# Bias of the mixing stage added by VectorE with the third product, in the first eight of twelve groups

## The chip, the cores and the metric

One core of a Trainium2 chip runs the whole kernel. Its engines work side by side, each through its own queue in a fixed order: TensorE (PE in the rows, its weight loads PEld), VectorE (DVE), ScalarE (ACT), GpSimd (POOL), and SyncE (SP), which issues most transfers. The metric is the device time of one execution in microseconds; of three runs of the kernel before, the median is 1185.93 us (1185.71 to 1186.15).

## The reference, cut to what matters

The input is `x`, two sequences of 3008 rows by 256. The first layer mixes in the frequency domain; two gated layers follow, each on all 6016 rows.

```python
X = np.fft.rfft(x, axis=1)
Xr, Xi = X.real, X.imag
Yr = Xr @ w_r - Xi @ w_i + b_r
Yi = Xr @ w_i + Xi @ w_r + b_i
Yr = np.sign(Yr) * np.maximum(np.abs(Yr) - lam, 0.0)     # lam = 0.01
Yi = np.sign(Yi) * np.maximum(np.abs(Yi) - lam, 0.0)
y = np.fft.irfft(Yr + 1j * Yi, n=3008, axis=1)
...
h = x @ w_in;   x = (h * np.clip(h + 3, 0, 6) / 6) @ w_out       # 256 -> 2048 -> 256
g = x @ w_gate; x = (g * sigmoid(g) * (x @ w_val)) @ w_out2      # 256 -> 1536 -> 256
```

The change lies in the two `+ b` terms.

## The kernel before, in words

**The stages.** From 0 to about 190 us the kernel does the first layer, and from group 8 on the first blocks of the second layer between its pieces. The rest, to 1185 us, is the two gated layers. The transform is split: `pre` makes a first transform of the rows (line 328 or 330), its results go to memory (`Bd`) and come back as tiles `z`; then twelve groups `(b, Q)`, six to a sequence, pass through three steps; the inverse of the first transform (`post`, line 573) reads what they wrote to memory (`Cd`).

**A group's three steps.** All matrices are kept as a high and a low part, so that a product is three matmuls (`xh·wl`, `xh·wh`, `xl·wh`).

- `s2` (two halves): line 397 makes the group's frequencies in PSUM. ScalarE copies one part out (`sum`, L403) and casts the high part (`X`, L404), VectorE forms the difference (L405) and the low part (L132). In the following step, `then` makes the high and low part of the difference (ScalarE L410, VectorE L132).
- `ln` (two halves, `h` = 0 and 1): the complex product with the weights in three real products of 2 x 3 matmuls each (L441 to L443). Two go to the two halves of the PSUM tile `p3`, the third to `p4`. Ahead of them line 446 fills `p3` with the bias (plus lam) by a product of `ones` with `shift`. ScalarE copies `p4` to `k1` (L452), VectorE adds it to both halves (`yb`, L454). In the following step, `then` does the threshold: ScalarE L459 makes `yc` from `yb`, VectorE L460 makes `yp` from both.
- `ia` (line 471): multiplies `yp` of both halves back; ScalarE copies the result to `cs` (L474), POOL sends it to `Cd`.

**What sets the order.** Nothing is scheduled by the machine: each engine's queue holds what the code issues, in that order. For groups 2 to 7 the order on TensorE is `ln(p,0)`, `s2(p+1)`, `ia(p-1)`, `ln(p,1)`, then the next group; `run` puts the deferred halves (`then`) of one step behind the matmuls of the next. `ln` also makes a step of `conv1.step()` in groups 1 to 7: it converts the second layer's weights from 64-bit words, with one or two ScalarE casts (L170, L191) and up to four short VectorE operations (L175, L188, L179, L195). `flush` then issues the deferred halves. So VectorE's queue holds, over and over: four conversions, `yb(p,0)`, the first half of `s2`, `yp(p,0)`, the second half, the low parts, four conversions, `yb(p,1)`, `yp(p,1)`.

**PSUM.** Eight banks are used in turn. From group 8 (`FROM`) on, five are left, since three hold sums of the second layer.

**SBUF.** `b_st`, which holds the bias as it comes from memory, is one of three buffers of the ring `r`, which also holds `yb` and `yc`. It is needed only until `shift` is made of it (L297, L298, L300).

Of the kernel before, what the change touches and what calls it, by code (L numbers as in the profile page):

```python
# [9 lines left out]
F32 = mybir.dt.float32  # L10
# [4 lines left out]
ALU = mybir.AluOpType  # L15
# [5 lines left out]
SEQ, DIM, NB = 3008, 256, 2  # L21
# [5 lines left out]
LAM = 0.01  # L27
# [58 lines left out]
def fourier_moe_kernel(ctx: ExitStack, tc: tile.TileContext, x, lin, bias, w1, w2, fwd1, inv2, fwd2,  # L86
                       inv1, out):
    nc = tc.nc

    def pool(stack, name, side):  # L90
        return stack.enter_context(tc.tile_pool(name=name, bufs=1, side=side))
# [39 lines left out]
    def low(o, full, hi):  # L131
        nc.vector.tensor_tensor(out=o, in0=full, in1=hi.bitcast(F32), op=ALU.subtract)  # L132
# [89 lines left out]
    ap_ = pool(attn_stack, "attn", "right")  # L222
    linh = ap_.tile([128, 3, 2, DIM], F32R, name="linh")
    linl = ap_.tile([128, 3, 2, DIM], F32R, name="linl")
    shift = ap_.tile([128, 2 * DIM], F32R, name="shift")
    ones = ap_.tile([128, 128], F32R, name="ones")
# [8 lines left out]
    def load_x(k):  # L235
        t, src = room[k], x[k * 2 // NT, k % (NT // 2)]
        if k == 0:
            for n in range(4):
                c = slice(n * TC // 2, (n + 1) * TC // 2)
                nc.sync.dma_start(t[:QP, c], src[:, c])  # L240
        else:
            nc.sync.dma_start(t[::2], src[:64])
            nc.sync.dma_start(t[1::4], src[64:])
# [17 lines left out]
    p = [psf[0]([128, 512], f"p0_{n}") for n in range(2)]  # L261
# [4 lines left out]

    def prepare():
        lin_st = ap_.tile([128, 2, 2, DIM], F32, tag="z", name="lin_st", bufs=3)
        b_st = spread("b_st")
        nc.gpsimd.dma_start(lin_st, lin)  # L270
        nc.gpsimd.dma_start(b_st[:64], bias)
        for h in range(2):
            nc.gpsimd.memset(room[5][:, h * TC : (h + 1) * TC], 0.0)
        load_x(5)
        load_m(0, 0)
        o = spread("o_st")[:, :128]
        nc.gpsimd.memset(o, 0.0)
        for r in (0, 32):
            nc.gpsimd.memset(o[r : r + 1], 1.0)
        nc.gpsimd.tensor_copy(ones, o)  # L280
        nc.gpsimd.tensor_copy(shift[64:], zeros[64:])
        w = [lin_st[:, k] for k in range(2)]

        def mixed(op):
            w.append(spread("mixed").rearrange("p (a b) -> p a b", b=DIM))
            nc.vector.tensor_tensor(out=w[-1], in0=w[1], in1=w[0], op=op)

        def hi(i, k):
            nc.scalar.copy(linh[:, i], w[k])

        def lo(i, k):
            low(linl[:, i], w[k], linh[:, i])

        def shifts(i):
            b = b_st[:64]
            if i == 0:
                nc.vector.tensor_scalar(b, b, LAM, None, op0=ALU.add)  # L297
                nc.scalar.copy(shift[:64], b)  # L298
            else:
                low(shift[32:64], b[32:], shift[32:64])  # L300

        amid.update({
            6: [lambda: mixed(ALU.subtract), lambda: hi(2, 0)], 7: [lambda: mixed(ALU.add), lambda: hi(0, 2)],
            8: [lambda: lo(2, 0), lambda: shifts(0)], 9: [lambda: lo(0, 2), lambda: hi(1, 3)],
            10: [lambda: lo(1, 3), lambda: shifts(1)]})

    amid = {}

    def spread(name):
        return xs_p.tile([128, 2 * DIM], F32, tag="r", name=name, bufs=3)  # L310
# [60 lines left out]
    def table(tag, src, Q, name, bufs):  # L371
        t = ap_.tile([128, 4, 128], F32, tag=tag, name=name, bufs=bufs)
        nc.sync.dma_start(t, src[:, Q * 512 : (Q + 1) * 512].rearrange("r (g c) -> r g c", g=4))
        return t

    def load_m(b, Q):
        if (b, Q) not in m_t:
            m_t[b, Q] = table("m", fwd2, Q, f"m{b}_{Q}", 3)
# [38 lines left out]
    def flush():  # L417
        while due:
            due.pop(0)()
# [8 lines left out]
    def ln(b, Q, h):  # L428

        if (b, Q) not in n_t:  # L430
            n_t[b, Q] = table("n", inv1, Q, f"n{b}_{Q}", 3)
        if 0 < ORDER.index((b, Q)) < FROM:
            conv1.step()
        flush()
        xs = [t[:, :, :, h * 128 : (h + 1) * 128] for t in X[b, Q]]

        def product(o, form, k, start):
            for dh in range(2):
                xh, xl = (t[:, dh, form] for t in xs)
                wh, wl = linh[:, k, dh], linl[:, k, dh]  # L440
                nc.tensor.matmul(o, xh, wl, start=start and dh == 0, stop=False, skip_group_check=not start)  # L441
                nc.tensor.matmul(o, xh, wh, start=False, stop=False, skip_group_check=not start)  # L442
                nc.tensor.matmul(o, xl, wh, start=False, stop=dh == 1, skip_group_check=not start)  # L443

        p = psf[0]([128, 2, DIM], f"p3_{b}_{Q}_{h}")
        nc.tensor.matmul(p.rearrange("r c d -> r (c d)"), ones, shift, start=True, stop=True)
        product(p[:, 1], 0, 0, False)
        product(p[:, 0], 1, 1, False)
        p1 = psf[0]([128, DIM], f"p4_{b}_{Q}_{h}")
        product(p1, 2, 2, True)  # L450
        k1 = ap_.tile([128, DIM], F32, tag="k1", name=f"k1{b}_{Q}_{h}", bufs=2)
        nc.scalar.copy(k1, p1)  # L452
        yb = xs_p.tile([128, 2, DIM], F32, tag="r", name=f"yb{b}_{Q}_{h}", bufs=3)
        nc.vector.tensor_tensor(out=yb, in0=p, in1=k1.unsqueeze(1).to_broadcast([128, 2, DIM]), op=ALU.add)  # L454
        yc = xs_p.tile([128, 2, DIM], F32, tag="r", name=f"yc{b}_{Q}_{h}", bufs=3)
        y = yp[b, Q, h] = ap_.tile([128, 2, DIM], F32, tag="yp", name=f"yp{b}_{Q}_{h}", bufs=3)

        def then():
            nc.scalar.activation(yc, yb, AF.Relu, bias=edges)  # L459
            nc.vector.scalar_tensor_tensor(out=y, in0=yb, scalar=0.0, in1=yc, op0=ALU.min, op1=ALU.add)  # L460

        later.append(then)
# [19 lines left out]
    ORDER = [(b, Q) for b in range(NB) for Q in range(NQ)]  # L482
    FROM = 8
# [11 lines left out]
    def L(p):  # L495
        return [lambda h=h: ln(*ORDER[p], h) for h in range(2)]
# [682 lines left out]
    for q in range(len(quads2) + 1):  # L1179
        if q < len(quads2) and quads2[q][1] == 0 and quads2[q][0] + 1 < len(pairs):  # L1180
            p = quads2[q][0] + 1
# [50 lines left out]
```

## Time and profile before

| | us |
|---|---|
| median of three runs | 1185.93 |
| the profiled execution's own time | 1187.32 |
| its span, first to last instruction | 1185.5 |
| TensorE busy in the span | 1176.2 (99%) |
| VectorE busy | 915.3 (77%) |
| ScalarE busy | 780.9 (66%) |

The page names TensorE as busy nearly all the time and puts 94% of the chain that ended last on it, under a granted clock of 1.00. Matmuls overlap in the profile: one has a duration of 280 or 400 ns, but the next starts after some 120 or 230 ns. What one matmul is worth is therefore read from the distance of starts or from the chain, not from its duration. The average also hides the stages: what holds TensorE up between 30 and 115 us is read from that stretch alone.

### The profile page before, as it was taken

To read this page: it belongs to the slowest core of one execution; us is meant where nothing else is said; L and a number is where in the kernel's file an instruction comes from. 1 tells how busy PE (TensorE), PEld (TensorE's weight loads), DVE (VectorE), ACT (ScalarE), POOL (GpSimd) and SP (SyncE) were. 2 spreads that over 40 slices of the span, in tenths; PEclk is the share of its full clock that TensorE was granted. 3 is DMA by queue.
4 is the path that set the end of the run, shared out by engine and by line. 5 is a ranking of instruction groups with operands and counts; after the bars stand their busy time and mean duration, and the time that the engine had idled before them with its cause. 6 is when DMAs were issued, how large, how long until landed. Compare 5 with 4: busy or idle time off the path is not lost.

```text
span 1185.5 us, 17927 instructions
## 1 busy us (share of the span) xinstructions
PE 1176.2 (99%) x6576; PEld 979.5 (83%) x6576; DVE 915.3 (77%) x1629; ACT 780.9 (66%) x1432; POOL 58.0 (5%) x91
## 2 busy tenths in 40 slices
PE   9999999999999999999999999999999999999998
PEld 3898887888888888888899888888888888888997
DVE  5688985898989989989987666766766766766665
ACT  3577775688777777777777555655655655655554
POOL 4010004500000000000000000000000000000000
PEclk9999999999999999999999999999999999999999
DMA  8898534964472673643553544644644644644551
GB/s 300 299 323 224 169 84 133 311 231 151 131 259 93 189 247 106 201 158 142 204 185 133 178 155 155 228 155 158 231 156 160 229 160 160 226 160 160 200 195 71
DMA packets 69208, 219.63 MB, mean 185 GB/s; under 512 B 6672, under 2 KB 29200, under 8 KB 57296
## 3 DMA queue, kind: packets, MB, share of 16 engines
q1 hardware_dynamic: 66144, 209.28, 51.4%
q0 software_dynamic: 2688, 9.05, 2.6%
q8 instruction: 51, 0.84, 0.3%
q14 instruction: 37, 0.30, 0.1%
q10 hardware_dynamic: 288, 0.16, 0.0%
HBM read 172.07 MB, written 46.40 MB: 184 GB/s over the span
## 4 chain that ended last, share of the span: by engine, by line
PE 94%; DVE 3%; DMA 2%; ACT 1%; issue 1%; POOL 0%; SPq 0%; ACTq 0%; POOLq 0%; DVEq 0%
PE acc L127 12%; PE acc L129 12%; PE acc L128 12%; PE P L933 8%; PE P L935 8%; PE P L934 8%; PE Tb L935 4%; PE Tb L933 4%; PE Tb L934 4%; PE Q L933 2%; PE Q L935 2%; PE Q L934 2%; PE p L471 2%; PE p L397 2%; PE p L442 1%; PE p L443 1%
## 5 line engine op out<-in xcount | busy, mean ns | idle before, releaser
L990 ACT COPY hold<-P 128x512 f32<-128x512 f32 (+1 forms) x224 | 128.7, 575 | 78.5 <-PE P L935 77.4
L613 ACT CAST gated<-r 128x512 fp32r<-128x512 f32 (+1 forms) x160 | 98.1, 613 | 64.9 <-DVE r L981 53.7
L132 DVE TENSOR_TENSOR gated<-s,gated 128x512 fp32r<-128x512 f32 (+1 forms) x144 | 97.4, 676 | 49.7 <-ACT gated L1117 49.7
L985 DVE TENSOR_TENSOR hold<-Q,hold 128x512 f32<-128x512 f32 (+1 forms) x112 | 76.1, 679 | 67.6 <-PE Q L935 55.3
L132 DVE TENSOR_TENSOR gated<-r,gated 128x512 fp32r<-128x512 f32 (+1 forms) x160 | 107.9, 674 | 21.6 <-ACT gated L613 18.3
L127 PE MATMUL acc<-gated,w_o 128*128 128x512 f32 (+1 forms) x320 | 123.9, 387 | 0.0
L128 PE MATMUL acc<-gated,w_o 128*128 128x512 f32 (+1 forms) x320 | 123.1, 385 | 0.0
L129 PE MATMUL acc<-gated,w_o 128*128 128x512 f32 (+1 forms) x320 | 123.0, 384 | 0.0
L129 PE MATMUL acc<-gated,slot 128*128 128x512 f32 (+1 forms) x288 | 111.1, 386 | 0.0
L127 PE MATMUL acc<-gated,slot 128*128 128x512 f32 (+1 forms) x288 | 111.0, 385 | 0.1
L128 PE MATMUL acc<-gated,slot 128*128 128x512 f32 (+1 forms) x288 | 110.9, 385 | 0.0
L985 DVE TENSOR_TENSOR hold<-P,hold 128x512 f32<-128x512 f32 (+1 forms) x112 | 75.8, 677 | 39.3 <-PE P L935 39.3
L1157 ACT ACTIVATE s<-hold 128x512 f32<-128x512 f32 (+1 forms) x72 | 44.9, 623 | 85.6 <-DVE hold L985 85.6
L977 ACT ACTIVATE r<-hold,consts 128x512 f32<-128x512 f32 (+1 forms) x120 | 85.7, 715 | 17.3 <-DVE hold L985 15.1
L985 DVE TENSOR_TENSOR hold<-Tb,hold 128x512 f32<-128x512 f32 (+1 forms) x112 | 76.0, 678 | 26.5 <-PE Tb L935 19.4
L933 PE MATMUL P<-xo,slot 128*128 128x512 f32 (+1 forms) x240 | 91.7, 382 | 0.2
L934 PE MATMUL P<-xo,slot 128*128 128x512 f32 (+1 forms) x240 | 91.5, 381 | 0.0
L935 PE MATMUL P<-xo,slot 128*128 128x512 f32 (+1 forms) x240 | 91.4, 381 | 0.0
L1117 ACT CAST gated<-s 128x512 fp32r<-128x512 f32 (+1 forms) x144 | 88.1, 612 | 1.5 <-DVE s L1172 1.2
L981 DVE SCALAR_TENSOR_TENSOR r<-r,hold 128x512 f32<-128x512 f32 (+1 forms) x120 | 80.9, 674 | 4.5 <-ACT r L977 3.4
L1162 ACT ACTIVATE s<-hold 128x512 f32<-128x512 f32 (+1 forms) x72 | 45.0, 625 | 51.5 <-DVE hold L985 51.5
L990 ACT COPY hold<-Tb 128x512 f32<-128x512 f32 (+1 forms) x112 | 64.8, 578 | 7.8 <-PE Tb L935 0.4
(190 smaller groups left out, 2865.8 us busy)
## 6 DMA issues: line engine op xcount, KB each, us to landing
slot<-Wd SPq DMA_DIRECT2D x72, 1152.0 KB, 5.1
slot<-Sd SPq DMA_DIRECT2D x40, 896.0 KB, 4.7
st<-in_w SPq DMA_DIRECT2D x68, 256.0 KB, 5.0
Wd<-slot SPq DMA_DIRECT2D x12, 1152.0 KB, 5.1
z<-Bd SPq DMA_DIRECT2D x12, 512.0 KB, 5.6
Cd<-cs POOLq DMA_DIRECT2D x24, 256.0 KB, 4.1
Xd<-x SPq DMA_DIRECT2D x20, 256.0 KB, 3.0
raw<-Xd SPq DMA_DIRECT2D x5, 1024.0 KB, 7.5
```

Of the source, the lines that this page charges most:

```text
L127: nc.tensor.matmul(o, wl, xh, start=start, stop=False)
L128: nc.tensor.matmul(o, wh, xh, start=False, stop=False)
L129: nc.tensor.matmul(o, wh, xl, start=False, stop=stop)
L132: nc.vector.tensor_tensor(out=o, in0=full, in1=hi.bitcast(F32), op=ALU.subtract)
L613: nc.scalar.copy(hi[:, :n], g[:, :n])
L933: nc.tensor.matmul(o, wl, x[m][:, 0, :n], start=start, stop=False, skip_group_check=not start)
L934: nc.tensor.matmul(o, wh, x[m][:, 1, :n], start=False, stop=False, skip_group_check=not start)
L935: nc.tensor.matmul(o, wh, x[m][:, 0, :n], start=False, stop=True, skip_group_check=not start)
L977: nc.scalar.activation(r[:, :n], x[:, :n], AF.Relu, bias=three)
L985: nc.vector.tensor_tensor(out=h, in0=x[:, :n], in1=c, op=ALU.add)
L990: nc.scalar.copy(c, x[:, :n])
L1117: nc.scalar.copy(hi[:, :nb], t[:, :nb])
```

## The change

In groups 0 to 7 (`early`) the product with `ones` is left out, and the first product into each half of `p3` starts its sum anew. ScalarE's copy of `p4` to `k1` is left out as well. Instead VectorE makes two additions where it made one: first `p4` (read twice, by broadcast) plus the bias plus lam, from SBUF, into `yb`; then `p3` plus `yb` into `yb`. For this the bias stays in SBUF on all 128 partitions, in a buffer of its own (`b_st` leaves the ring `r`), and the array on the host has 128 equal rows instead of 64. Groups 8 to 11 are as before, so `ones` and `shift` are still made.

```diff
     def prepare():
-        b_st = spread("b_st")
+        b_st = ap_.tile([128, 2 * DIM], F32, name="b_st")
+        edge_b.append(b_st.rearrange("p (c d) -> p c d", d=DIM))
         nc.gpsimd.dma_start(lin_st, lin)
-        nc.gpsimd.dma_start(b_st[:64], bias)
+        nc.gpsimd.dma_start(b_st, bias)
...
-                nc.vector.tensor_scalar(b, b, LAM, None, op0=ALU.add)
+                nc.vector.tensor_scalar(b_st, b_st, LAM, None, op0=ALU.add)
                 nc.scalar.copy(shift[:64], b)
...
         p = psf[0]([128, 2, DIM], f"p3_{b}_{Q}_{h}")
-        nc.tensor.matmul(p.rearrange("r c d -> r (c d)"), ones, shift, start=True, stop=True)
-        product(p[:, 1], 0, 0, False)
-        product(p[:, 0], 1, 1, False)
+        early = ORDER.index((b, Q)) < FROM
+        if not early:
+            nc.tensor.matmul(p.rearrange("r c d -> r (c d)"), ones, shift, start=True, stop=True)
+        product(p[:, 1], 0, 0, early)
+        product(p[:, 0], 1, 1, early)
         p1 = psf[0]([128, DIM], f"p4_{b}_{Q}_{h}")
         product(p1, 2, 2, True)
-        k1 = ap_.tile([128, DIM], F32, tag="k1", name=f"k1{b}_{Q}_{h}", bufs=2)
-        nc.scalar.copy(k1, p1)
         yb = xs_p.tile([128, 2, DIM], F32, tag="r", name=f"yb{b}_{Q}_{h}", bufs=3)
-        nc.vector.tensor_tensor(out=yb, in0=p, in1=k1.unsqueeze(1).to_broadcast([128, 2, DIM]), op=ALU.add)
+        if early:
+            nc.vector.tensor_tensor(out=yb, in0=p1.unsqueeze(1).to_broadcast([128, 2, DIM]), in1=edge_b[0], op=ALU.add)
+            nc.vector.tensor_tensor(out=yb, in0=p, in1=yb, op=ALU.add)
+        else:
+            k1 = ap_.tile([128, DIM], F32, tag="k1", name=f"k1{b}_{Q}_{h}", bufs=2)
+            nc.scalar.copy(k1, p1)
+            nc.vector.tensor_tensor(out=yb, in0=p, in1=k1.unsqueeze(1).to_broadcast([128, 2, DIM]), op=ALU.add)
```

VectorE's queue in the kernel before, from the second half of group 4 to the first half of group 5 (names end in sequence, group and half; `wt`, `head`, `st` and `w1` belong to the conversion of weights):

```order
L454 TENSOR_TENSOR yb0_4_1_891<-p3_0_4_1_868,k10_4_1_889 128x512
L460 SCALAR_TENSOR_TENSOR yp0_4_1_894<-yb0_4_1_891,yc0_4_1_893 128x512
L195 TENSOR_TENSOR w1_c_733<-wt_735,w1_c_733 128x256
L175 TENSOR_SCALAR wt_902<-head_864 128x256
L188 SCALAR_TENSOR_TENSOR wt_860<-head_781,wt_860 128x256
L179 SCALAR_TENSOR_TENSOR wt_902<-st_741,wt_902 128x256
L454 TENSOR_TENSOR yb0_5_0_933<-p3_0_5_0_910,k10_5_0_931 128x512
```

The same place in the changed kernel:

```order
L456 TENSOR_TENSOR yb0_4_1_870<-p4_0_4_1_863,b_st_161 128x512
L457 TENSOR_TENSOR yb0_4_1_870<-p3_0_4_1_850,yb0_4_1_870 128x512
L467 SCALAR_TENSOR_TENSOR yp0_4_1_874<-yb0_4_1_870,yc0_4_1_873 128x512
L195 TENSOR_TENSOR w1_c_719<-wt_721,w1_c_719 128x256
L175 TENSOR_SCALAR wt_882<-head_846 128x256
L188 SCALAR_TENSOR_TENSOR wt_842<-head_765,wt_842 128x256
L179 SCALAR_TENSOR_TENSOR wt_882<-st_727,wt_882 128x256
L456 TENSOR_TENSOR yb0_5_0_910<-p4_0_5_0_903,b_st_161 128x512
L457 TENSOR_TENSOR yb0_5_0_910<-p3_0_5_0_890,yb0_5_0_910 128x512
```

Nothing changes its place on VectorE; each `yb` has become two rows, the second of which reads what the first wrote.

TensorE's queue in the kernel before, where `ia` of group 3 ends and `ln` of group 4 begins its second half:

```order
L471 MATMUL p5_0_3_0_842<-yp0_3_1_769,n0_3_650 128x256
L471 MATMUL p5_0_3_1_843<-yp0_3_1_769,n0_3_650 128x256
L446 MATMUL p3_0_4_1_868<-shift_121,ones_122 128x512
L441 MATMUL p3_0_4_1_868<-linl_120,X0_4_691 128x256
L442 MATMUL p3_0_4_1_868<-linh_119,X0_4_691 128x256
```

In the changed kernel:

```order
L478 MATMUL p5_0_3_0_824<-yp0_3_1_753,n0_3_638 128x256
L478 MATMUL p5_0_3_1_825<-yp0_3_1_753,n0_3_638 128x256
L442 MATMUL p3_0_4_1_850<-linl_120,X0_4_677 128x256
L443 MATMUL p3_0_4_1_850<-linh_119,X0_4_677 128x256
L444 MATMUL p3_0_4_1_850<-linh_119,X0_4_677 128x256
```

The row of 512 columns is gone, and the group's first product of 256 columns follows `ia` directly.

## Rows read from the trace of the kernel before

**Rows 1.** The page, busy us of each engine, share of the span, instructions.
```profile
PE 1176.2 (99%) x6576; PEld 979.5 (83%) x6576; DVE 915.3 (77%) x1629; ACT 780.9 (66%) x1432; POOL 58.0 (5%) x91
```

**Rows 2.** Busy time by stretch of one group (us, instructions), granted clock, DMA share, GB/s.
```profile
54.30:64.80 10.50, 10.50 (x78) 8.79 (x77) 6.86 (x14) 6.78 (x16) 1.80 (x3) 1.00 0.99 327
82.20:90.90 8.70, 8.70 (x73) 8.02 (x72) 7.67 (x19) 6.57 (x18) 1.26 (x2) 1.00 1.00 336
99.60:108.30 8.70, 8.70 (x72) 7.89 (x70) 7.62 (x18) 6.40 (x17) 1.26 (x2) 1.00 0.95 185
```

**Rows 3.** One line's instructions: count, ns min/median/max, first and last start, form.
```profile
L446 PE MATMUL p<-shift,ones x24: 389/400/793, 32.8 to 178.6; 128*128 128x512 f32 x24
...
L452 ACT COPY k<-p x24: 351/373/394, 35.8 to 181.2; 128x256 f32<-128x256 f32 x24
...
L454 DVE TENSOR_TENSOR yb<-p,k x24: 681/691/693, 36.2 to 181.6; 128x512 f32<-128x512 f32 x24
...
L297 DVE TENSOR_SCALAR b_st<-b_st x1: 411/411/411, 24.2 to 24.2; 64x512 f32<-64x512 f32 x1
```

**Rows 4.** The chain that ended last, by time: start us, us on the chain, what.
```profile
31.10 5.96 DMA z<-Bd
...
79.73 0.23 PE p L446
79.96 0.12 PE p L441
...
85.83 0.43 PE p L446
```

**Rows 5.** VectorE's timeline: start us, us, line, operation, [idle before <- releaser].
```profile
61.54 0.36 DVE L175 TENSOR_SCALAR wt<-head 128x256 uint32<-128x256 uint32 x1
61.94 0.42 DVE L179 SCALAR_TENSOR_TENSOR wt<-st,wt 128x256 uint32<-128x256 uint32 x1
...
80.17 0.69 DVE L454 TENSOR_TENSOR yb<-p,k 128x512 f32<-128x512 f32 x1
81.66 0.69 DVE L460 SCALAR_TENSOR_TENSOR yp<-yb,yc 128x512 f32<-128x512 f32 x1 [0.79 <-ACT yc L459]
...
83.47 0.68 DVE L454 TENSOR_TENSOR yb<-p,k 128x512 f32<-128x512 f32 x1
84.07 0.41 DVE L405 TENSOR_TENSOR sum<-p,sum 128x256 f32<-128x256 f32 x1
...
88.86 0.69 DVE L454 TENSOR_TENSOR yb<-p,k 128x512 f32<-128x512 f32 x1
```

**Rows 6.** Who VectorE waited for, 60 to 115 us: total us, times, longest.
```profile
DVE yp L460 <- ACT yc L459: 4.7, 6, 0.8
DVE X L132 <- ACT X L410: 2.8, 6, 1.1
DVE xa L132 <- ACT xa L586: 0.8, 1, 0.8
DVE yb L454 <- ACT k L452: 0.6, 2, 0.4
DVE sum L405 <- ACT X L404: 0.5, 2, 0.3
```

**Rows 7.** TensorE's timeline where the transform of `post` ends; columns as in rows 5.
```profile
113.05 0.50 PE L129 MATMUL ph<-xa,w_c 128*128 128x512 f32 x1 [0.20 <-DVE xa L132]
```

**Rows 8.** ScalarE's timeline in group 4; columns as in rows 5.
```profile
80.90 0.73 ACT L459 ACTIVATE yc<-yb,consts 128x512 f32<-128x512 f32 x1 [0.76 <-DVE yb L454]
86.82 0.43 ACT L410 CAST X<-sum 128x256 fp32r<-128x256 f32 x1
```

**Rows 9.** The chain at the end of the first layer; columns as in rows 4.
```profile
186.63 1.98 PE p L471 x16
188.60 1.07 ACT cs L474 x2
...
190.58 3.71 DMA Cd<-cs
...
195.46 0.50 PE acc L127
```

**Rows 10.** VectorE's timeline, a slower operation of the same size later; columns as in rows 5.
```profile
215.03 0.96 DVE L132 TENSOR_TENSOR gs<-r,gs 128x512 fp32r<-128x512 f32 x1 [1.69 <-ACT gs L613]
```

More of the change, by code (lines that the diff above doesn't have):

```diff
@@ L305, in prepare @@
             10: [lambda: lo(1, 3), lambda: shifts(1)]})
-    amid = {}
+    amid, edge_b = {}, []
     def spread(name):
@@ L1193 @@
     xp = np.pad(xp, ((0, 0), (0, QP - QN), (0, 0))).reshape(NB, QP, NJ // 8, 8 * DIM).transpose(0, 2, 1, 3)
-    bias = np.tile(np.concatenate([b_r, b_i]), (64, 1))
+    bias = np.tile(np.concatenate([b_r, b_i]), (128, 1))
     def rows(w):
```

## The prediction

> **What bounds the kernel now.** I read the page's busy times first: TensorE 99%, its weight loads 83%, VectorE 77% [rows 1]. That is an average over stages, and the changed instructions all lie between 32 and 108 us, so the next view is the busy time by stretches of one group, to see who has room there. In every stretch TensorE is busy throughout and the granted clock is 1.00. VectorE goes from 6.86 of 10.50 us in an early stretch to 7.67 of 8.70 in a later one [rows 2]. The chain by time shows how TensorE's work lines up: up to 37.1 us it waits for a transfer, from then on one matmul follows the other, 0.12 us for one of 256 columns and 0.23 us for the product with ones [rows 4]. VectorE's timeline and the list of its waits then show what its apparent room consists of [rows 5, 6], and TensorE's timeline after the last changed group shows the place that decides: at 113.05 us TensorE itself waits for VectorE's `xa` [rows 7]. So at that point the two engines meet. TensorE sets the pace up to there, but VectorE arrives at the end of the stretch a little later than TensorE, and whatever shifts VectorE's arrival shifts everything after it.
>
> **What is removed from TensorE.** 16 of the 24 products with ones go [rows 3]: eight groups, two halves. Each takes 0.23 us of the chain. Where it follows `ia` it has 0.43 [rows 4], but the 0.20 more is the change from 64 rows to 128, which the next product then pays. 16 x 0.23 = 3.7 us; the first falls ahead of the wait for `z`, which ends at 37.06 whatever TensorE does [rows 4], so 15 x 0.23 = 3.5 us at most are a gain.
>
> **What is removed from ScalarE.** 16 copies of 0.37 us [rows 3], 5.9 us of busy time. ScalarE is not the bound; what counts is that VectorE's `yb` no longer waits for this copy. In 60 to 115 us it did so twice, 0.6 us together [rows 6].
>
> **What is added to VectorE.** 16 additions of 128x512 that read one operand from PSUM and one from SBUF. `yb` in the trace is that form, with the broadcast on the other operand: 0.69 us [rows 3]. Two operations that don't depend on each other overlap a little (83.47 to 84.07, a distance of 0.60), but the second addition reads what the first wrote. The pair L175 and L179 shows such a dependence: the first ends at 61.90, the second begins at 61.94 [rows 5]. So an added one costs 0.69 + 0.03 = 0.72 us of VectorE's queue. No row shows a broadcast read from PSUM. The bounds are the nearest rows: 0.41 (half the columns) from below [rows 5], 0.96 (the same size, slowed later on) from above [rows 10]. I take 0.72, the same form. Nothing excludes that it is hidden, only that it is negative: the operation is new, and nothing on VectorE goes.
>
> The Trainium skill says in "VectorE: DVE Perf Modes", section "The DRAIN you can't avoid", that a semaphore between chained operations costs nothing extra, since the next one waits for the pipeline anyway. The dependent pair above begins 0.04 us after the end of the first, the independent one 0.08 before it, so here the trace differs by about 0.12 each. By that rule eleven additions would cost 1.3 us less than in the sum below, and the result would be 1189.9.
>
> **Where VectorE hides it and where not.** In groups 0 to 2 there is cover: 3.6 of 10.5 us idle around group 2 [rows 2], and TensorE keeps its lead. The cover ends at about 61 us. From then on the queue has the four weight conversions in each half of a group, and I count from the second half of group 2 to the second half of group 7: 11 added operations, 11 x 0.72 = 7.9 us. In 60 to 115 us VectorE waits for 9.4 us [rows 6]. Most of this is no cover:
> - 4.7 us are six waits of `yp` for ScalarE's `yc`, which is made from `yb` just before (0.79 each). When `yb` comes later, so does `yc` (it starts 0.04 us after `yb` ends [rows 5, 8]). These stay.
> - 2.8 us are waits for ScalarE's cast L410. The longest, 1.1, ends at 61.2, ahead of the first counted operation; 1.7 are left. ScalarE's queue is in order, with that cast behind `yc` and two copies [rows 8], so it too moves with `yb`. 0.5 us more wait for L404. Of these 2.2 I let 0.3 go.
> - 0.6 us for the copy `k` go with it, and 0.8 us for `xa` go, since ScalarE's cast no longer arrives last when VectorE is late.
>
> So 0.6 + 0.8 + 0.3 = 1.7 us disappear. A lead is to be taken off as well: when the stretch begins, TensorE has left out four products since 37.1 us, 4 x 0.23 = 0.9, and VectorE, which waits at 61.2 for ScalarE and through it for TensorE, starts earlier by that much.
>
> **The sum.** VectorE's arrival at `xa`: 7.9 - 1.7 - 0.9 = +5.3 us. TensorE, ready earlier by 3.5 us, waits there and on the way there for `yp` and `X`, about 8.8 us more than before. A check on one group: `yb` of groups 4 and 5 are 8.69 us apart [rows 5]; with two additions the distance becomes 10.1, while TensorE needs 8.70 - 0.46 = 8.24. What is late next is therefore `yp` for `ia` and the low part of `X` for `ln`, both from VectorE.
>
> After 113 us the order and the work are the old ones, so the shift is carried on: at the end of the layer the last `ia` goes through ScalarE's copy and a transfer of 3.71 us to TensorE's next wait [rows 9], and nothing there can make up for a late `ia`. What else is touched costs nothing: the bias is loaded to 128 rows instead of 64, early, and VectorE reads it at 24.2 us without having waited [rows 3]. `b_st`'s leaving the ring frees a buffer. Several TensorE and ScalarE rows have one more semaphore to wait for, all of long-past work.
>
> The profiled execution took 1187.32 us, 1.8 more than its span and 1.4 more than the median of the runs. With +5.3 it would be 1192.6. Against the median 1185.93 this is **1191.2 us**. With the bounds of the addition: 11 x 0.41 - 2.6 = +1.9 (1187.8), and 11 x 0.99 - 2.6 = +8.3 (1194.2). If all the 2.2 us of L410 and L404 go, the sum is +3.4 (1189.3).
>
> **Rivals.**
> - *TensorE is the bound and VectorE hides all* (chance 0.07). For it: TensorE's 99%, and VectorE's 9.4 us of waits, which are more than 7.9. Then 15 x 0.23 = 3.5 us are gained: 1182.4, faster. It needs the 4.7 us of waits for `yc` to be usable, against an in-order queue, and the wait at 113.05 to go with them. The Trainium skill, "Perfetto Trace Analysis", section "Identifying the Most-Contended Engine", takes the engine with the highest occupancy as the one to relieve, for TensorE by its weight loads: 83% against VectorE's 77% also points to TensorE, and so to this rival; the rows by stretch speak against it here.
> - *Part is hidden* (0.09). Additions follow at a distance of 0.60, and all the waits for L410 and L404 turn into cover: 6.6 - 0.6 - 0.8 - 2.2 - 0.9 = +2.1, 1188.0, inside what can't be told from no change.
> - *More is lost* (0.10). VectorE's lateness also holds the weight conversions, whose buffers the loads on SP's queue wait for, and the loads of `z` stand behind these. Or the addition is as slow as its upper bound: 1194.2. It decides where a group's `z` lands later than VectorE's `X` of the group before; the DMA share is 1.00 in one stretch [rows 2].
> - The forecast (0.74).
>
> **How the numbers follow.** About 0.2%, 2.4 us, is what a measurement of this kernel can tell from no change. Slower by more: the forecast without 0.02 of its tail, and the third rival, 0.82. Within: the second and that tail, 0.11. Faster: 0.07. The range 1187.0 to 1194.0 leaves out the first rival, the lower half of the second and the upper half of the third, less than 2 in 10.
>
> **What would show it.** The line of `yb` splits in two with 16 operations each at about 0.69, the second 0.72 after the first; the product with ones is left 8 times. In the stretches of groups 4 to 7 the distance of `yb` to `yb` is about 10.1 us, and VectorE's only larger waits are those for `yc` and L410. TensorE, busy throughout before, shows gaps of 0.4 to 2 us ended by VectorE at L441 to L443, L471 and L573, about 9 us in all between 70 and 118; `xa` ends 5.3 us later, and so do the last `ia` and the end. I would be wrong if TensorE's gaps stayed away while VectorE has its 16 operations more (the first rival), if the second addition took much less than 0.6, or if the shift at 118 us were not found again at the end.

## The result and the profile after

The changed kernel takes 1195.03 us, median of four runs (1193.33 to 1196.14); beside it the kernel before took 1186.04 (1185.71 to 1186.97). The ratio is 1.0066 with a 95% interval of 1.0054 to 1.0078, that is 7.8 us with 6.4 to 9.3 around it; the two medians differ by 9.0. So it is slower, as forecast, but by more than the 5.3 us of the forecast. The median lies 1.0 us above the upper end of the stated range; the ratio, applied to the 1185.93 us from which the forecast was worked out, gives 1193.8 us, just inside it. The profiled run took 1193.33 us and its span is 1191.6, 6.0 more than before.

The page's busy times, as in [rows 1]: TensorE has 16 instructions less, VectorE 16 more, ScalarE 16 less.

```profile
PE 1175.3 (99%) x6560; PEld 978.1 (82%) x6560; DVE 925.1 (78%) x1645; ACT 774.5 (65%) x1416; POOL 58.2 (5%) x91
```

Busy time by stretch, as in [rows 2]: an early one, then group 4 from `yb` to `yb`, then a later one.

```profile
54.30:64.80 10.50, 10.50 (x90) 9.73 (x91) 8.41 (x19) 6.15 (x14) 1.80 (x3) 1.00 0.99 329
81.80:92.20 10.40, 9.35 (x78) 8.68 (x78) 9.01 (x20) 6.09 (x15) 1.26 (x2) 1.00 1.05 380
99.00:109.50 10.50, 9.40 (x72) 8.18 (x71) 9.53 (x22) 5.44 (x14) 0.13 (x1) 1.00 0.92 168
```

TensorE, which had no idle time in any stretch of [rows 2], is now idle for a tenth of a group, and VectorE is busy for 9.0 to 9.5 us of a group that used to take 8.7. (In the middle stretch TensorE's idle time is a wait for `z`, in the last one it is a wait for VectorE's `X`; see below.) The two engines have changed places.

The lines that answer to [rows 3]: both additions, and what is left of the products with ones.

```profile
L456 DVE TENSOR_TENSOR yb<-p,b_st x16: 674/683/692, 35.3 to 111.4; 128x512 f32<-128x512 f32 x16
...
L457 DVE TENSOR_TENSOR yb<-p,yb x16: 690/691/692, 36.1 to 112.1; 128x512 f32<-128x512 f32 x16
...
L449 PE MATMUL p<-shift,ones x8: 389/389/396, 107.6 to 184.6; 128*128 128x512 f32 x8
```

VectorE's timeline, as in [rows 5]: the start of the stretch without cover, then group 4 up to the first `yb` of group 5.

```profile
59.56 0.36 DVE L175 TENSOR_SCALAR wt<-head 128x256 uint32<-128x256 uint32 x1
...
78.91 0.42 DVE L195 TENSOR_TENSOR w_c<-wt,w_c 128x256 fp32r<-128x256 f32 x1
...
80.11 0.68 DVE L456 TENSOR_TENSOR yb<-p,b_st 128x512 f32<-128x512 f32 x1
80.83 0.69 DVE L457 TENSOR_TENSOR yb<-p,yb 128x512 f32<-128x512 f32 x1
82.37 0.69 DVE L467 SCALAR_TENSOR_TENSOR yp<-yb,yc 128x512 f32<-128x512 f32 x1 [0.85 <-ACT yc L466]
...
84.90 0.69 DVE L457 TENSOR_TENSOR yb<-p,yb 128x512 f32<-128x512 f32 x1
85.51 0.41 DVE L406 TENSOR_TENSOR sum<-p,sum 128x256 f32<-128x256 f32 x1
...
90.32 0.68 DVE L456 TENSOR_TENSOR yb<-p,b_st 128x512 f32<-128x512 f32 x1
```

The second addition begins 0.72 us after the first (80.11 to 80.83); the independent one behind it follows after 0.61 (84.90 to 85.51). From `yb` to `yb` it is 10.21 us (80.11 to 90.32), where it was 8.69 [rows 5].

Who VectorE waited for between 60 and 122 us, as in [rows 6].

```profile
DVE yp L467 <- ACT yc L466: 5.1, 6, 0.8
DVE X L132 <- ACT X L411: 1.5, 5, 0.6
DVE xa L132 <- ACT xa L593: 0.8, 1, 0.8
DVE sum L406 <- ACT X L405: 0.3, 1, 0.3
```

The waits for `yc` did not shrink, they grew a little. Only the wait for `k` went, and some tenths of those for L411 and L405; 0.8 us before `xa` is still there. No wait for a transfer is in the list.

Where TensorE now stands still for over 0.3 us between 70 and 116 us (the bracket: idle time before the instruction, and what ended it).

```profile
72.86 2.02 PE L398 MATMUL p<-m,z 128*128 128x128 f32 x16 [2.34 <-DMA z<-Bd]
82.85 2.02 PE L398 MATMUL p<-m,z 128*128 128x128 f32 x16 [1.54 <-DMA z<-Bd]
98.70 0.39 PE L442 MATMUL p<-linl,X 128*128 128x256 f32 x1 [0.64 <-ACT X L405]
99.75 0.39 PE L444 MATMUL p<-linh,X 128*128 128x256 f32 x1 [0.56 <-DVE X L132]
109.31 0.38 PE L444 MATMUL p<-linh,X 128*128 128x256 f32 x1 [0.55 <-DVE X L132]
112.92 0.28 PE L580 MATMUL p<-inv_sb,ct 48*64 48x47 f32 x2 [0.37 <-DVE yb L457]
114.97 1.34 PE L580 MATMUL p<-inv_sb,ct 48*64 48x47 f32 x67 [1.77 <-DVE yb L461]
```

Half of this, 3.9 of 7.8 us, is ended by the transfer of `z`, not by VectorE. The rest is VectorE's (L405's too: it is late because the queue ahead of it is). The last two are in `post`, whose matmuls wait for banks that VectorE's `yb` still reads.

Then comes something that the forecast has no term for. Three stretches of 2 us behind that last wait (the granted clock is the third number from the end):

```profile
114.00:116.00 2.00, 1.03 (x67) 1.03 (x68) 2.00 (x4) 1.54 (x3) 0.00 (x0) 0.97 1.05 411
116.00:118.00 2.00, 2.00 (x34) 1.72 (x30) 1.22 (x3) 1.13 (x3) 0.00 (x0) 0.50 1.04 383
118.00:120.00 2.00, 2.00 (x10) 1.67 (x10) 2.00 (x7) 0.92 (x4) 0.00 (x0) 0.68 0.36 126
```

The granted clock falls to 0.50, 1.2 GHz, and comes back to 2.4 GHz before 120 us: (0.03 + 0.50 + 0.32) x 2 us / 0.5 = 3.4 us at half speed. In the kernel before it is 1.00 here.

Follow the shift to the end. VectorE's two pairs of `xa` in the kernel before (first fence) and the second pair after (second fence):

```profile
110.50 1.29 DVE L132 TENSOR_TENSOR xa<-p,xa 128x512 fp32r<-128x512 f32 x2 [0.77 <-ACT xa L586]
112.31 1.28 DVE L132 TENSOR_TENSOR xa<-p,xa 128x512 fp32r<-128x512 f32 x2
```

```profile
117.49 1.29 DVE L132 TENSOR_TENSOR xa<-p,xa 128x512 fp32r<-128x512 f32 x2 [0.78 <-ACT xa L593]
```

The chain after, an early piece and then those that answer to [rows 9]:

```profile
30.66 5.20 DMA z<-Bd
...
192.64 1.98 PE p L478 x16
194.62 1.06 ACT cs L481 x2
...
196.59 3.72 DMA Cd<-cs
...
201.48 0.50 PE acc L127
```

The second `xa` pair is 5.18 us later (112.31 to 117.49), the forecast's 5.3. But the last `ia` is 6.01 later (186.63 [rows 9] to 192.64), and this stays to the end. The chain itself has moved as well: where it ran over TensorE alone in the kernel before (from 37 to 110 us, pieces of it in [rows 4]), its pieces between 69 and 114 us are now mostly VectorE's and ScalarE's. One of them is a transfer of weights (`st`, 7.09 us at 82.32), but in that time VectorE stands still only for `yc` and for L411. And one detail flatters the 5.18: in this run the first transfer of `z` ended at 35.86, in the kernel before at 37.06 [rows 4]; TensorE began the groups 1.20 us earlier for a reason that has nothing to do with VectorE's sum.

How far `z` can shift a profile by itself is seen in g1 below, whose edits lie behind `post`. There TensorE waits for a later `z` twice, for 1.75 us in the row below and for 1.53 us at 85.20, and the second `xa` pair is 3.20 us later than in the kernel before, without a change on VectorE:

```profile
74.74 2.02 PE L397 MATMUL p<-m,z 128*128 128x128 f32 x16 [1.75 <-DMA z<-Bd]
```

### The profile page after: what moved, and what is told of

It is laid out like the page before. It is cut to its first block, busy times and chain, and to the rows that moved or that the text cites. A ratio compares the mean times of both kernels' runs of the same rounds, so it can differ in the third digit from the quotient of the medians.

```text
span 1191.6 us, 17921 instructions
## 1 busy us (share of the span) xinstructions
PE 1175.3 (99%) x6560; PEld 978.1 (82%) x6560; DVE 925.1 (78%) x1645; ACT 774.5 (65%) x1416; POOL 58.2 (5%) x91
## 4 chain that ended last, share of the span: by engine, by line
PE 90%; DVE 4%; DMA 3%; ACT 2%; issue 1%; SPq 0%; POOL 0%; ACTq 0%; POOLq 0%; DVEq 0%
PE acc L127 12%; PE acc L129 12%; PE acc L128 12%; PE P L940 8%; PE P L941 8%; PE P L942 8%; PE Tb L942 4%; PE Tb L940 4%; PE Tb L941 4%; PE Q L940 2%; PE Q L942 2%; PE Q L941 2%; PE p L331 1%; PE p L580 1%; PE p L478 1%; PE ph L127 1%
```

## The experiments

Three sets, each on one chip with the kernel before beside it (medians 1187.68, 1187.76 and 1187.11 us); ratios are against that. The theory was first that VectorE's queue is the whole price; from the second set on, that falls of TensorE's granted clock are added to it.

**How many groups.** The changed kernel with the early form in the first three, or the first six groups.

```
-        early = ORDER.index((b, Q)) < FROM
+        early = ORDER.index((b, Q)) < 3        # e4_groups_0_5: < 6
```

> The change in groups 0 to 2 only (6 products with ones out, 6 additions in). Theory (VectorE's queue is full from about 61 us on and its arrival at xa decides): all six additions lie where VectorE has cover, the count of added operations behind 61 us falls from 11 to 1, so the time is that of the kernel before or up to 0.9 us less (1185.0 to 1186.2), no gap of TensorE on VectorE before xa, and the granted clock stays at 1.00 throughout. Rival (TensorE pays for something in every group, whatever VectorE does): three eighths of the whole change's loss of 9, so about +3.4 us. Rival (the loss is one event, a fall of the clock, not a sum over groups): either +0 or all of it.

> The change in groups 0 to 5 (12 products out, 12 additions in). Theory (per group with full weight conversions VectorE's period grows from 8.7 to about 10.2 us): 7 added operations behind 61 us, 5.0 less 1.7 and less 0.9 to 2 of lead: +1.4 to +2.4 us at xa; with a fall of the clock after it up to 0.9 more for one of 3.4 us. Rival (equal shares per group): six eighths of 9, +6.7. Rival (only the clock counts): the time depends on whether TensorE's gaps of about 1 us are enough for the clock to fall, all or nothing.

Measured: three groups 1187.59 us, ratio 0.9997 (0.9984 to 1.0010); six groups 1191.26, ratio 1.0024 (1.0011 to 1.0037), +2.8 us; all eight were 1.0066. The second `xa` pair is late by 0.86, 3.24 and 5.18 us. So the cost isn't per addition: the first six are free, and the price grows from about 61 us on, where the prediction put the end of the cover. The 0.86 of the three groups is not VectorE's: in that profile TensorE waits 1.25 and 1.12 us for `z` at 72.91 and 82.95. The 3.24 of the six groups lies above the 1.4 to 2.4 us that were expected; seven additions of 0.72 are 5.04, TensorE's lead was 1.06 (L175 at 60.48), so by difference only 0.74 of VectorE's waits went, where the expectation had let 1.7 go.

**One side of the trade alone.** e2 keeps the products with ones and still adds twice on VectorE (the added operand is a tile of zeros); e3 leaves out the products in groups 0 to 7 and changes nothing on VectorE.

```
 e2, against the changed kernel:
-        if not early:
-            nc.tensor.matmul(p..., ones, shift, start=True, stop=True)
-        product(p[:, 1], 0, 0, early)
+        nc.tensor.matmul(p..., ones, shift, start=True, stop=True)
+        product(p[:, 1], 0, 0, False)
 e3, against the kernel before:
-        nc.tensor.matmul(p..., ones, shift, start=True, stop=True)
-        product(p[:, 1], 0, 0, False)
+        if not early:
+            nc.tensor.matmul(p..., ones, shift, start=True, stop=True)
+        product(p[:, 1], 0, 0, early)
```

> VectorE's cost alone: the changed kernel with the product with ones kept in all groups; the operand that VectorE adds to the third product is zero instead of the bias. Theory (VectorE decides): 11 x 0.72 = 7.9 us less 1.7 of waits that go, and no lead of TensorE: +6.2 against before up to xa, so within 1 us of the changed kernel although TensorE has 3.7 us more work; behind it the granted clock may or may not fall, since TensorE's gaps are shorter by 3.7 us (a fall of some 3.4 us costs 0.9). Rival (TensorE is the bound and each product counts): the changed kernel's time plus 3.7, 1198.7.

> TensorE's part alone: the kernel before without the product with ones in groups 0 to 7; the copy of the third product and VectorE's one addition stay. The bias of these groups is left out of the result. Theory (at xa the two engines meet, and VectorE's chain has no work less): 0 to -0.9 us against before (1185.0 to 1186.0), with TensorE waiting for VectorE at xa. Rival (TensorE is the bound): 15 x 0.23 = -3.5 us, 1182.5.

Measured: e2 1196.16 us, ratio 1.0066 (1.0047 to 1.0086); e3 1188.26, ratio 1.0004 (0.9987 to 1.0021). The additions alone cost as much as the whole change. In e2's profile, with `z` at its old time (37.07), the second `xa` pair is 6.90 us late, 6.2 were expected. The 3.5 us taken from the engine that is busy for 99% of the time are by themselves worth nothing that can be measured: a gain of 0 to 0.9 us was expected, and in e3's profile the second `xa` pair comes 1.09 us later than before. There TensorE runs ahead into the transfer of `z`, and then into a fall of its clock (its timeline, and two stretches):

```profile
73.16 2.20 PE L397 MATMUL p<-m,z 128*128 128x128 f32 x13 [2.52 <-DMA z<-Bd]
```

```profile
72.00:74.00 2.00, 0.84 (x7) 0.87 (x8) 0.91 (x2) 0.00 (x0) 0.00 (x0) 1.00 1.04 250
74.00:77.60 3.60, 3.60 (x19) 3.12 (x19) 2.29 (x5) 2.64 (x6) 0.00 (x0) 0.53 0.87 304
```

**VectorE relieved of something else.** One of two conversion steps in groups 3 to 7 goes behind `post` (reckoned at 1.45 us of VectorE each); f3 is the changed kernel with this, f4 the kernel before.

```
-        if 0 < ORDER.index((b, Q)) < FROM:
+        if 0 < ORDER.index((b, Q)) < FROM and not (h == 1 and ORDER.index((b, Q)) > 2):
             conv1.step()
...
-        for _ in range(2 - n % 2):
+        for _ in range(2):
```

> The changed kernel, with one of the two conversion steps of a group (shift, two logical operations and a subtraction on VectorE, 1.45 us) left out in groups 3 to 7 and made up behind post, two steps in each unit: 5 x 1.45 = 7.2 us less on VectorE before xa, nothing else taken away, TensorE's 3.5 us saved as in the changed kernel. Theory (VectorE's sum up to post is the whole price of the change): the shift of xa against before goes from +5.2 to between -2 and +0.5, where the wait for z and TensorE's own sum stand, and the time is 1184 to 1188 (ratio 0.998 to 1.001). Rival (the price is the wait for z or for freed banks, which the second addition merely lengthens): xa stays 3 us or more late and the time above 1190.

> The kernel before with the same move of five conversion steps, so that fewer operations of VectorE and fewer loads stand before post. Theory (TensorE bounds the kernel before up to post; its VectorE has slack of a few us): no change, ratio 0.999 to 1.001, xa at 113.6 within 0.7 us. Rival (VectorE or the loads already bound the kernel before): xa 2 to 5 us earlier and the ratio 0.996 to 0.998.

The second `xa` pair in f3, then in f4:

```profile
111.88 1.28 DVE L132 TENSOR_TENSOR xa<-p,xa 128x512 fp32r<-128x512 f32 x2
```

```profile
111.06 1.28 DVE L132 TENSOR_TENSOR xa<-p,xa 128x512 fp32r<-128x512 f32 x2
```

Up to `post` the theory holds: `xa` of the changed kernel goes from +5.18 to -0.43 us, 5.6 earlier. My 7.2 us counted durations (the four operations of a step last 1.55 us together); operations overlap, and a step takes 1.20 us of the queue (78.91 to 80.11 in the timeline above), five of them 6.0. The same relief moves the kernel before by -1.25 only, 0.9 of it from `z`, which was earlier: that kernel was not held up by VectorE up to there. Between f3 and f4 0.82 us are left of the change's 5.18. As a whole both expectations missed: f3 took 1192.36 us, ratio 1.0037 (1.0025 to 1.0049), f4 1189.82, ratio 1.0022 (1.0013 to 1.0032). In both the steps made up behind `post` cost 3.8 us between the first `xa` pair and the last `ia`. There was no room for them. In f4 the chain that ended last runs over VectorE and ScalarE from 115 to 175 us, where it ran over TensorE in the kernel before, and TensorE waits for their `gs`. How the 3.8 us are made up was not taken apart.

**TensorE kept busy in the wait.** The changed kernel with nine products whose result nobody reads, ahead of the part of `post` that waits.

```
         o = [psf[0]([128, BLK], f"p6_{p}_{t}_{eh}") for t in range(2)]
+        if (p, eh) == (0, 1):
+            idle = acc_bank([128, 2 * DIM], "idle")
+            for _ in range(9):
+                nc.tensor.matmul(idle, ones, shift, start=True, stop=True)
         inverse(o, p, eh)
```

> The changed kernel, with nine products of 128x512 (ones by the shift, into a bank that nobody reads) on TensorE between the two parts of post, where the changed kernel's TensorE waited 0.37 and 1.77 us for VectorE's yb; 9 x 0.23 = 2.1 us, so they end where that wait ended. Theory (the granted clock falls because TensorE had stood still there): the clock stays at 1.00 between 112 and 120 us, the shift against before at the last L478 is that at xa (+5.2, in the changed kernel +6.0), and the profiled span is about 0.8 us shorter, 1190.8 where nothing falls elsewhere. Rival (the fall belongs to this stretch whatever TensorE does in the wait, or the idle products delay post): 0.5 still stands at 116 us, or xa ends later than 118.8 by more than 0.3, and the span stays at 1191.6 or above.

TensorE's timeline there, and the same three stretches:

```profile
113.74 2.35 PE L589 MATMUL idle<-shift,ones 128*128 128x512 f32 x9
116.02 1.70 PE L580 MATMUL p<-inv_sb,ct 48*64 48x47 f32 x88
```

```profile
114.00:116.00 2.00, 2.00 (x9) 1.34 (x8) 1.15 (x3) 1.87 (x4) 0.00 (x0) 1.00 1.06 413
116.00:118.00 2.00, 2.00 (x91) 1.86 (x91) 1.97 (x4) 1.05 (x3) 0.00 (x0) 1.00 1.04 399
118.00:120.00 2.00, 2.00 (x11) 1.31 (x10) 1.62 (x4) 1.48 (x4) 0.00 (x0) 1.00 0.92 331
```

The clock stays at 1.00. Here `z` ended as late as in the kernel before (its first matmul at 37.10, there 37.09), so this profile gives VectorE's price: the second `xa` pair +6.07, the last `ia` +6.08. It does wait 1.46 us for a later `z` (at 73.17); g2, which has the same edit up to there, a first `z` at 37.12 and no later wait for one, shows that this costs nothing, with +6.05 and +6.07. The second `xa` pair in f1, then in g2:

```profile
118.38 1.29 DVE L132 TENSOR_TENSOR xa<-p,xa 128x512 fp32r<-128x512 f32 x2 [0.41 <-ACT xa L597]
```

```profile
118.36 1.29 DVE L132 TENSOR_TENSOR xa<-p,xa 128x512 fp32r<-128x512 f32 x2 [0.41 <-ACT xa L597]
```

So VectorE's additions, less TensorE's lead, cost 6.1 us against a kernel before that does not wait for a later `z`. The span isn't shorter than the changed kernel's, as was expected, but equal (1191.6): 0.8 us less for the clock, 1.2 more for `z`, and the expectation had not reckoned with the latter. By `xa` alone (0.9 later than in the changed kernel) the rival's sign was met, for that same reason. The time, 1192.90 us, ratio 1.0047 (1.0034 to 1.0059), is lower than the changed kernel's, but the intervals overlap.

**The stand at 195 us.** Before and after the change TensorE stands for 1.88 us where the last group's `cs` is written to memory. The reason is in the tiles: the first block's results (ScalarE's `x`) are written where `cs` is still being read. f5 is the kernel before with these in another ring; g1 adds to it that the sums of the second stage's weights come two units later; g2 is the changed kernel with both and with the idle products.

```
+        if k == blocks[0]:
+            pool_, tag = xs_p, "r"
         o = pool_.tile([128, BLK], F32, tag=tag, name="x2", bufs=3)
...
-        u = 4 * j // 3
+        u = 4 * j // 3 + 2                     # g1 and g2 only
```

> The kernel before with one edit elsewhere: the first block's two results (L605, L607) go into the ring r, whose place is free, and not into a tile that lies where the last group's cs is still being read by the transfer Cd<-cs. Theory (TensorE's stand of 1.88 us at 195 us is that wait, and the falls of the granted clock behind it come from the stand): the stand goes or is below 0.5 us, the time is 1.3 to 1.9 us shorter (ratio 0.9985 to 0.999) and fewer runs have a mean clock below 1.0. Rival (the ring's three buffers take the place of the wait): a stand of 1 us or more remains around 195 us and the ratio is 1.000.

> The kernel before, with the first block's results in the ring r (as in f5_first_rows_in_r) and also the sums of the second stage's weights (L752 there) two units later, so that nothing on VectorE or ScalarE behind post waits for the last transfer Cd<-cs. Theory (TensorE's stand of 1.88 us at 195 us is a wait of VectorE's and ScalarE's queues for that transfer, and a stand of that length is what the granted clock falls after): no stand above 0.4 us there, every run at a mean clock of 0.999 or 1.000, ratio 0.997 to 0.9985 (1.9 us of stand, and about 1.6 us of a fall in the runs that had one). Rival (the ring or the later sums give it back): a stand of 1 us or more between 190 and 215 us, ratio 0.999 to 1.000.

> The changed kernel with the idle products of f1_idle_products and both edits of g1_no_stand: the same additions, but TensorE stands still neither in post nor at 201 us. Theory (of the change's cost VectorE's additions carry 5 to 6 us, and the rest are falls of the granted clock after stands): mean clocks 0.999 or 1.000, and 4.8 to 6.2 us above g1_no_stand (ratio of the two 1.004 to 1.0052). Rival (the rest is something else that the additions bring): 7 us or more above g1_no_stand.

TensorE's stands over 0.3 us behind 190 us, in f5 and then in g1:

```profile
195.87 0.50 PE L129 MATMUL acc<-gs,w_o 128*128 128x512 f32 x1 [1.20 <-DVE gs L132]
```

```profile
231.42 0.50 PE L129 MATMUL acc<-gs,w_o 128*128 128x512 f32 x1 [0.85 <-DVE gs L132]
237.51 0.50 PE L127 MATMUL acc<-gs,w_o 128*128 128x512 f32 x1 [0.50 <-ACT gs L615]
242.53 0.50 PE L935 MATMUL P<-xo,slot 128*128 128x512 f32 x1 [0.35 <-ACT hold L992]
```

f5: 1186.41 us, ratio 0.9991 (0.9983 to 1.0000). A stand of 1.20 us is left, as the rival had it, but not because of the ring: a sum on VectorE waits for the same transfer. The mean clock was 1.000 in 7 of its 11 runs and 0.999 in the rest; the kernel before had 1.000 in one of 21 and 0.998 in 16. It is the fastest version tried here, but its interval touches 1. g1: 1188.37 us, ratio 1.0008 (0.9999 to 1.0017). The stand at 195 is gone and the clocks are 0.999 or 1.000, but the later sums give it back 35 us further on, 1.7 us in three pieces. That is the rival's cause, though later and in smaller pieces than it said; theory's shorter time missed. g2: 1195.03 us, ratio 1.0064 (1.0052 to 1.0076), 6.7 us above g1, between what theory and rival said, and three of its five runs have a mean clock of 0.997 or 0.998, where 0.999 or 1.000 were expected. The comparison of times settles nothing; g2's profile, with a clock of 1.00 throughout, is the one used above.

**The changed kernel once more.**

> The changed kernel once more, beside the two others on one chip. Theory: a stand of 1.6 to 1.9 us in post and one of 1.88 at 201 us, a fall of the granted clock after one or both, mean clocks 0.995 to 0.998, ratio 1.0054 to 1.0078 as measured before. Rival: without a fall in its profile and still 7 us or more above the kernel before.

Measured: 1194.91 us (1191.63 to 1196.40), ratio 1.0057 (1.0044 to 1.0070), mean clocks 0.995 (three runs) to 0.999. Its profile has two falls. The wait in `post` and the stretches behind it, then the one behind the stand at 203 us:

```profile
114.84 2.58 PE L580 MATMUL p<-inv_sb,ct 48*64 48x47 f32 x86 [1.77 <-DVE yb L461]
```

```profile
114.00:116.00 2.00, 1.16 (x44) 1.17 (x48) 2.00 (x5) 1.41 (x3) 0.00 (x0) 0.70 1.03 400
116.00:118.00 2.00, 2.00 (x56) 1.82 (x49) 0.57 (x1) 0.54 (x2) 0.00 (x0) 0.50 0.95 339
118.00:120.00 2.00, 2.00 (x6) 1.59 (x5) 1.92 (x5) 1.18 (x4) 0.00 (x0) 0.50 0.08 28
120.00:122.00 2.00, 2.00 (x11) 1.88 (x10) 2.00 (x7) 1.40 (x4) 0.00 (x0) 0.59 0.18 20
203.50:207.00 3.50, 3.50 (x10) 2.73 (x9) 2.31 (x4) 1.37 (x3) 3.39 (x5) 0.51 0.90 322
```

The two profiles of the same program and that of f1, against the kernel before (us; "next `inverse`" is the first of its matmuls behind 190 us, at 199.10 in the kernel before):

| | second `xa` pair | last `ia` | next `inverse` | span | time at half clock |
|---|---|---|---|---|---|
| f1, idle products | +6.07 | +6.08 | +6.07 | +6.1 | none |
| changed, first profile | +5.18 | +6.01 | +6.03 | +6.0 | 3.4 |
| changed, second profile | +5.77 | +7.45 | +9.05 | +9.1 | 6.8 and 3.4 |

Without a fall the shift at `xa` is the shift at the end. With falls it grows: by 0.83 and 1.68 us between `xa` and the last `ia`, and by 1.60 more for the one at 204 us. Where in the runs without a profile the falls lie is not known. But the changed kernel's runs with the lowest mean clocks are its longest (0.995: 1196.10 to 1196.40 us; 0.998 and 0.999: 1191.63 to 1193.71), so the 7.8 us of the ratio and the 9.0 between the medians fit a mixture of the two cases in the table.

## Why the prediction was right, and where not

- *Direction and mechanism up to `xa`: right.* VectorE's queue between 61 and 113 us sets the end of the stretch; e2 alone reproduces the whole cost, e3 shows that TensorE's side alone gains nothing, and f3 removes the shift at `xa` by relieving VectorE elsewhere. *That 5.3 us were forecast for the shift and 5.18 measured is luck:* a miss of about 1 us in the waits and a `z` that happened to come 1.20 us earlier, both below, cancel.
- *0.72 us for an addition, and 10.1 us from `yb` to `yb`: right* (0.72 and 10.21). The dependent addition follows 0.11 us later than the independent one. So the rule of the Trainium skill in "VectorE: DVE Perf Modes", section "The DRAIN you can't avoid", by which the wait for the operation before costs nothing extra, doesn't hold for this pair.
- *End of the cover, and the lead: right.* Up to three groups are free (e1). L175 at the start of the stretch came 1.98 us earlier (61.54 [rows 5] to 59.56); without the 1.20 of `z` it is 0.8, predicted 0.9. The 0.83 us between e2 (+6.90) and f1 (+6.07) are that lead too.
- *The waits that go, 1.7 us: mis-sized, it was 0.7 to 1.1.* From L175 at the start of the stretch to the second `xa` pair VectorE's waits sum to 8.46 us in the timeline before and to 7.71 after, so 0.75 went. The 0.8 us before `xa`, which I let go, stayed: ScalarE's cast is fed by a TensorE that was itself held up by VectorE's `yb`. With 0.75 instead of 1.7 and the lead of 1.98 that this profile had, the sum is 7.92 - 0.75 - 1.98 = +5.19, as measured. In f1, with `z` at its old time, the lead is 0.77 and by difference 1.08 of waits go: 7.92 - 1.08 - 0.77 = +6.07. The first profile hid the miss behind its earlier `z`.
- *"After 113 us the order and the work are the old ones, so the shift is carried on": this step failed.* The work is the same, but not the speed: behind the new wait in `post`, and in the second profile behind the stand of 1.89 us that the kernel before has too, the granted clock falls to 0.50. That is 0.8 to 3.3 us which the sum had no term for. It brings the time to the upper end of the range by the ratio, and past it by the median; that the one lies inside is owed to the width of the range and not to the sum.
- *TensorE's gaps, "about 9 us in all", "ended by VectorE": the amount fits* (7.8), *the cause only by half.* The waits for `z` weren't foreseen. They cost nothing here, since VectorE is later still (f1 has one and g2 has none, with the same `xa`). In e3 the wait for `z` of 2.52 us and the fall behind it stand where TensorE's saving should be. Late transfers of `z` are not the change's doing alone, since g1 has them too.
- *The rivals.* "TensorE is the bound": refuted by the result and by e3. The rule of the Trainium skill, "Perfetto Trace Analysis", section "Identifying the Most-Contended Engine", that pointed to it would still name TensorE by the page after (99%, weight loads 82%, VectorE 78%), in a kernel that VectorE now holds up. "Part is hidden" (1188.0): refuted by the time, and the waits for L410 and L404 went only in part. "More is lost" had the better size, but not by its mechanism: a late `z` is there, and VectorE is not held by it.

Open is why the same program falls in one run for 3.4 us and in another for 6.8, and why the kernel before, with its stand of 1.88 us, shows a mean clock of 0.998 in most runs of two sets (16 of 21, 10 of 17) and no fall in its own profile. 0.998 is the mean in the profiles of e4 and f3, each with one fall of 3.4 us.

## What to carry over

An engine that is busy for 78% of the whole can be full in the stretch that counts: before giving it work, count its queue from one end of that stretch to the other, and count waits that come from its own results as work, not as room. Work taken from the engine that is busy for 99% gains only up to the next floor, in e3 the transfer of `z`. Since `z` lands at another time in each run, compare more than one profile before a shift of 1 to 3 us is put down to a change. And where a change makes TensorE stand still, look for the granted clock behind the stand: a shift need not arrive at the end as it started.

## What the hardware showed that I had not expected

The granted clock fell to 1.2 GHz in the middle of a kernel whose TensorE is busy for 99% of the time, each time after TensorE had stood still. Behind 1.77 us in `post` it fell in all three profiles with that stand (twice in the changed kernel, once in e2); in f1 and g2, where the wait was filled, it stayed at 2.4 GHz. It fell after 2.52 us for `z` in e3. After the stand of 1.86 to 1.89 us at 195 to 204 us it fell in five profiles (e2, e3, e4, f3, g3) and did not in four (the kernel before, the changed kernel's first, e1, f1), nor after 2.34 us at 72.86 in the changed kernel. In f5 and g1, where that stand is 1.20 us or gone, none of 22 runs has a mean clock below 0.999. So a fall behind such a stand is likely here, not certain. A fall of 3.4 us at about 200 us cost 1.6 us of time in each of the five, one of 3.4 us behind `post` 0.8 (the changed kernel) and 1.3 (e2).
